# Second batch's transposed x in two PSUM banks, and a new order of the opening, in an attention and MLP kernel

## The chip, the cores and the metric

The kernel runs on one core of one Trainium2 chip. The metric is the device time of one execution in microseconds (us); the time before is the median of three runs. Profiles are of one execution, and times in them count from the start of its span. Engines: PE multiplies matrices, ACT and DVE do element-wise work and copies out of PSUM, POOL does element-wise work in SBUF and issues the loads, SP issues stores and transposing DMAs.

## The reference

```python
B, H, S, Ns, D = (8, 8, 512, 32, 64)
scores = scale * x @ state^T            # softmax over the 32 states
xread  = softmax(scores) @ state        # 512 token rows per batch
scores2 = scale * state @ x^T           # softmax over the 512 tokens
sread  = softmax(scores2) @ x           # 32 state rows per batch
attn   = concatenate([xread, sread], rows), heads side by side   # (8 * 544, 512)
h = attn @ w_in                         # 512 -> 2048
g = maximum(h, 0) + alpha * minimum(h, 0)
out = g @ w_out                         # 2048 -> 512, f32
```

## The kernel before, in words

Everything is computed in f16 with f32 sums. The token rows don't form xread: for each batch, state times w_in is formed first (`state_w_in`, step `m.b.f`, one of four column groups f) and copied to SBUF (`mo.b.f.engine.half`); the softmax weights then multiply it (`first`, step `F.b.jc`, sixteen column blocks jc, two matmuls each; `f.b.jc.g` is one half of such a step, so that it can start when half of the weights are there). `negative` (`N`) on ACT and `prelu` (`G`) on DVE apply the PReLU, and `second` (step `S.b.q.j`, two matmuls each) sums over the blocks with w_out for one of four groups of rows q; `second_out` (`O`) copies the sum and stores it. The state rows of all batches go through `state_reads` (`rd`) and stand as a ninth batch at the end (`F.8.*`, `R`).

Per batch, x is transposed, either by PE (`xt.b.j.g`, four transposes into PSUM, then a copy `xo`; batches 0 and 1) or by a DMA from SP (`xd`; batches 2 to 7). `sc` forms the scores. The softmax over states is `sb` (32x32 transposes, DVE), `smax`, `ssh` (POOL), `sexp` (ACT), `ssum`, `snorm` (POOL), `wb` (DVE, transposes back); F needs `wb`. The softmax over tokens is `tm`, `te` (ACT), `tsum`, `tn` (POOL), `tt` (transposing DMA from SP, read by `rd`). Batch 0 does the first of these in two halves (`sb.0.0`, `sb.0.1`).

Loads are issued on POOL's queue, in its order with its other work: x of batch 0 in halves (`lx0.0`, `lx0.1`), the states of batches 1 to 7 (`lst`), w_in in four column groups (`wi.0` to `wi.3`; `m.b.f` needs `wi.f`), w_out in four row groups (`wo.0` to `wo.3`; `S.b.q.0` and `.1` need `wo.0`, `.2` and `.3` `wo.1`, and so on), x of the later batches (`lx.b`).

The states of batch 0 come by SP, are cast (`stc`), transposed on PE (`stt`, needs the identity `id` that POOL makes) and copied (`sto`); those of the others are transposed in two groups (`str.0`, `str.1`) and copied on ACT (`sro`). `oma` on DVE makes 1 - alpha. `Z.k.n` are filler matmuls of zeros on PE, n units of 128 columns into PSUM bank k, whose result nobody reads.

The order is written out by hand: the string ORDER (L17 to L102) lists the steps, and every engine executes its own steps in that order. A number at the end of a step is the PSUM bank it uses (0 to 5); one further pair of banks ("two") holds `sc` and the `m` without numbers. A step that uses a bank waits until the reader of what stood there is done. The semaphores are set by the framework.

Of the kernel before, what the change touches and what calls it, by code (L numbers as in the profile page):

```python
# [46 lines left out]
S.1.3.5 N.2.8 S.1.3.6 G.2.7 F.2.6.2 O.1.0.a N.2.6 m.3.3.1.0 G.2.8 sc.4 rd.1.5 snorm.p.3 F.2.5.3
G.2.6 mo.3.3.a.0 F.2.14.1 rdo.1.a wb.3 N.2.5 tsum.3 S.2.1.0.2 F.2.11.5 mo.3.3.a.1 G.2.5 S.1.3.7
N.2.14 F.2.10.0 F.3.4.3 G.2.14 N.2.11 S.2.1.1 F.3.1.1 lx.5 O.1.3.v N.3.4 S.2.1.2 N.2.10 G.2.11 tt.2
S.2.0.0.4 S.2.1.3 S.2.0.1 G.2.10 F.3.14.5 F.3.9.0 S.2.1.4 tn.3.1 N.3.1 N.3.9 G.3.1 S.2.1.5 S.2.0.2  # L50
G.3.4 tn.3.0 N.3.14 tm.4 F.3.3.1 F.3.8.3 G.3.14 N.3.8 G.3.9 S.2.1.6 S.2.1.7 S.2.0.3 S.2.3.0.5 N.3.3
xd.5 O.2.1.a tt.3 sb.4 G.3.8 smax.4 F.3.6.0 F.3.2.2 te.4.0 S.2.3.1 S.2.3.2 N.3.6 N.3.2 F.3.13.3
S.2.0.4 te.4.1 ssh.p.4 N.3.13 G.3.3 G.3.6 S.2.0.5 F.3.7.1 G.3.2 S.2.0.6 N.3.7 S.2.0.7 sexp.4 G.3.13
G.3.7 S.2.3.3 S.2.3.4 S.2.3.5 m.6.0 O.2.0.v m.5.1.0.2 mo.6.0.a.1 mo.5.1.a.1 rd.3.3 mo.6.0.v.0
rdo.3.a mo.5.1.v.0 rd.2.1 m.4.1.4.2 ssum.4 sc.5 m.4.3.0.3 rdo.2.a S.2.3.6 mo.4.1.a.1 mo.4.1.a.0 tm.5
tsum.4 snorm.p.4 F.3.5.1 mo.4.3.a.0 mo.4.3.a.1 F.3.0.2 F.3.10.4 N.3.0 S.2.3.7 O.2.3.a S.2.2.0.0
S.2.2.1 F.3.11.3 G.3.0 wb.4 S.2.2.2 S.3.3.0.5 F.3.15.2 S.3.3.1 N.3.5 lx.6 G.3.5 te.5.0 te.5.1 N.3.10
N.3.15 S.2.2.3 F.3.12.1 S.2.2.4 N.3.11 S.3.3.2 lx.7 N.3.12 G.3.10 G.3.15 F.4.6.4 N.4.6 tn.4.0
# [583 lines left out]
```

## Time and profile before

| what | us |
|---|---|
| median of 3 runs (218.33 to 218.44) | 218.37 |
| the profiled execution | 218.92 |
| its span in the profile | 217.1 |
| PE busy in the span | 210.2 |
| DVE busy | 166.7 |
| ACT busy | 137.2 |
| POOL busy | 71.0 |
| matmuls of zeros (L218), busy | 7.3 |

The profile gives a page, and answers to questions about the trace: busy time of every engine in a stretch (windows), what an engine waited for (waits), groups of instructions with count, busy time and mean duration in ns, instructions in order of time (start, duration, engine, line, operation; in brackets the idle time of the engine before it and what ended that), DMA issues with their time to landing, and the chain of work that ended last. PE's matmuls are pipelined: a single one of 512 columns is shown as 379 ns long, but they follow each other more closely, as the chain shows.

### The profile page before, as it was taken

What the parts mean: (1) busy time and instruction counts of PE and PEld (TensorE: products, weight loads), DVE (VectorE), ACT (ScalarE), POOL (GpSimd) and SP (SyncE); (2) the same over time, 40 slices, a digit from 0 to 9 for tenths busy, and PEclk for the clock granted to TensorE, in tenths of its full rate; (3) what the DMA queues carried; (4) which work ended last, traced back from release to release, by engine and by line L of the source; (5) the groups of instructions that cost most, each with busy time, mean ns of one, the idle gap of its engine ahead of it and who ended that gap; (6) DMA issues with size and microseconds to landing.
All of it is one profiled execution on the core that took longest, in us unless ns stands there. A gap on an engine that the chain in (4) does not pass through costs nothing.

```text
span 217.1 us, 4195 instructions
## 1 busy us (share of the span) xinstructions
PE 210.2 (97%) x1637; PEld 99.8 (46%) x1637; DVE 166.7 (77%) x255; ACT 137.2 (63%) x271; POOL 71.0 (33%) x58
## 2 busy tenths in 40 slices
...
DMA packets 39716, 23.12 MB, mean 106 GB/s; under 512 B 22144, under 2 KB 35984, under 8 KB 39696
## 3 DMA queue, kind: packets, MB, share of 16 engines
...
q10 hardware_dynamic: 32, 0.01, 0.0%
...
## 4 chain that ended last, share of the span: by engine, by line
PE 85%; DMA 8%; POOL 2%; DVE 2%; issue 1%; ACT 0%; POOLq 0%
PE o L532 48%; PE h L480 23%; DMA w_in_sb<-in_moe_w_in_dram 6%; PE h L489 3%; PE o L580 3%; PE m_ps L447 3%; DMA st<-in_state_dram 3%; PE o L552 2%; PE sr_ps L422 2%; POOL an L358 1%; PE sc L297 1%; DVE m L469 1%; POOL xg L179 1%; DVE nb L378 1%; POOL w_in_sb L198 0%
## 5 line engine op out<-in xcount | busy, mean ns | idle before, releaser
L532 PE MATMUL o<-w_out_sb,gt 128*128 128x512 f16 x496 | 125.3, 379 | 0.0
L512 ACT ACTIVATE neg<-h 128x512 f32<-128x512 f32 (+1 forms) x144 | 77.0, 579 | 46.9 <-PE h L480 37.4
L520 DVE SCALAR_TENSOR_TENSOR gt<-neg,oma_sb,h 128x512 f16<-128x512 f32 x128 | 89.9, 738 | 15.5 <-ACT neg L512 14.5
L532 PEld LDWEIGHTS <-gt 128*128 128x128 f16 x496 | 47.3, 98 | 55.3 <-issue 3.4
L480 PE MATMUL h<-aT,m 128*128 128x512 f16 x250 | 68.4, 379 | 0.0
L480 PEld LDWEIGHTS <-m 128*128 128x128 f16 x250 | 24.1, 98 | 28.4 <-issue 0.6
L403 POOL TENSOR_SCALAR e<-e,r 128x512 f16<-128x512 f16 x16 | 24.9, 1564 | 20.6 <-DVE r L399 16.7
L469 ACT CAST m<-m_ps 128x512 f16<-128x512 f32 x50 | 27.1, 609 | 4.8 <-PE m_ps L447 4.5
L358 POOL TENSOR_TENSOR an<-ts,r 128x1024 f16<-128x1024 f32 (+1 forms) x9 | 15.4, 1718 | 34.2 <-DVE r L355 14.8
L344 POOL TENSOR_TENSOR ts<-ts,mx 128x1024 f32<-128x1024 f32 (+1 forms) x9 | 15.5, 1719 | 29.0 <-DVE mx L338 29.0
L570 ACT COPY osb<-o 128x512 f32<-128x512 f32 x22 | 12.9, 592 | 14.9 <-PE o L532 14.9
L447 PE MATMUL m_ps<-w_in_sb,stT 64*32 64x512 f16 x256 | 11.4, 383 | 0.8 <-DMA w_in_sb<-in_moe_w_in_dram 0.6
L389 ACT ACTIVATE e<-sc,nb 128x512 f16<-128x512 f32 x16 | 11.1, 703 | 1.1 <-DVE nb L381 1.1
L366 DVE STREAM_TRANSPOSE aT<-an 128x1024 f16<-128x1024 f16 (+1 forms) x9 | 10.1, 1119 | 1.8 <-POOL an L358 1.8
L469 DVE CAST m<-m_ps 128x512 f16<-128x512 f32 x14 | 9.1, 679 | 2.4 <-ACT m L469 1.8
L520 DVE SCALAR_TENSOR_TENSOR gs<-neg,oma_sb,h 128x256 f16<-128x256 f32 x16 | 7.5, 478 | 4.5 <-ACT neg L512 4.5
L378 DVE TENSOR_REDUCE nb<-sc 128x2 f32<-128x1024 f32 x8 | 9.6, 1204 | 0.3 <-PE sc L297 0.3
L338 DVE TENSOR_REDUCE mx<-ts 128x32 f32<-128x1024 f32 (+1 forms) x9 | 9.8, 1092 | 0.0
L354 DVE TENSOR_REDUCE r<-ts 128x32 f32<-128x1024 f32 (+1 forms) x9 | 9.8, 1088 | 0.0
L489 PE MATMUL h<-XS,w_in_sb 128*128 128x256 f16 x64 | 9.4, 273 | 0.0
L590 DVE COPY osr<-o 128x512 f32<-128x512 f32 x1 | 0.7, 691 | 11.3 <-PE o L580 11.3
L218 PE MATMUL z<-zero 128*128 128x512 f16 (+3 forms) x21 | 7.3, 481 | 1.6 <-DVE zero L211 1.3
...
## 6 DMA issues: line engine op xcount, KB each, us to landing
...
xg<-in_x_dram POOLq DMA_DIRECT2D x7, 512.0 KB, 7.0
w_in_sb<-in_moe_w_in_dram POOLq DMA_DIRECT2D x4, 512.0 KB, 9.7
w_out_sb<-in_moe_w_out_dram POOLq DMA_DIRECT2D x4, 512.0 KB, 8.4
...
```

The source lines that it names most:

```text
L344: engine(e).tensor_tensor(ts, ts, over_blocks(cols(live["mx", b], j, S // N)), ALU.subtract)
L358: engine(e).tensor_tensor(blocks(cols(live["an", b], j, S)), blocks(cols(live["ts", b], j, S)), over_blocks(cols(live["r1", b], j, S // N) ...
L378: nc.vector.tensor_reduce(nb, live["sc", b].rearrange("p r j g s -> p g (r j) s"), AX.XY, ALU.max)
L403: nc.gpsimd.tensor_scalar_mul(e2, e2, live["r2", b][:, g : g + 1])
L447: nc.tensor.matmul(t[N * k : N * (k + 1), :], st_head(b, h)[64 * r : 64 * r + 64, :], w_in_sb[64 * r : 64 * r + 64, c, 512 * f : 512 * (f ...
L469: copier(e)(m_tile(b)[:, f, g, :], live["mp", b, f][g])
L480: nc.tensor.matmul(h.rearrange("p (r j s) -> p r j s", r=2, j=2), ms[b][:, f, g, 128 * j : 128 * (j + 1)], weights(b, g), start=(g == 0), ...
L489: nc.tensor.matmul(h, w_in_sb[:, c, 128 * jc : 128 * (jc + 1)], XS[:, c].rearrange("p q n b -> p (q n b)"), start=(c == 0), stop=(c == n_c ...
L512: nc.scalar.activation(neg, h, RELU, bias=0.0, scale=-1.0)
L520: nc.vector.scalar_tensor_tensor(gt, negs.pop((b, jc)), oma_sb[:, jc : jc + 1], h, ALU.mult, ALU.add)
L532: nc.tensor.matmul(outs[b, q], gts[b, jc][:, 128 * q : 128 * (q + 1)], w_out_sb[:, jc, :], start=(jc == 0), stop=(jc == n_jc - 1),)
L570: copier(e)(osb, t)
```

## The change

x of batch 1 is transposed into two PSUM tiles of 1024 f16 columns (one bank each, both j in one) where there were four of 512, and each is copied with one DVE copy (`xo2.1.0.v`, `xo2.1.1.v`) in place of two. The order of all engines is written anew from the start up to about the third batch's first steps; the steps from there on have the same order, with the bank numbers exchanged. In the opening, among others: the identity is made behind `lst` and `wi.0`; `sto` goes to DVE and stands ahead of `oma`; one copy of batch 0's x goes from DVE to ACT; `wo.0` is issued ahead of `ssh.p.0.0`, `wi.2` ahead of both `snorm.p.0`, and `wo.2`, `lx.2` and `wo.3` ahead of `tn.0.0` and `tn.0.1`; `tt.0` is behind three stores on SP; the fillers are 32, 6, 3, 6, 28 and 6 units where they were 24, 13, 6, 3, 7 and 23; `m.4.0` comes ahead of the first `f`.

```diff
@@ ORDER @@
-stc lx0.0 lx0.1 oma id Z.1.24 stt.0 Z.2.13 xt.0.0.0.1 sto.a xt.0.1.0.2 xo.0.0.0.v lst xo.0.1.0.v
-Z.0.6 sc.0.0 xt.0.1.1.3 xt.0.0.1.4 sb.0.0 xo.0.0.1.v smax.0.0 xo.0.1.1.a str.0.5 sc.0.1 str.1.0 wi.0
-sro.0.a lx.1 wi.1 ssh.p.0.0 sb.0.1 Z.1.3 sc.0 Z.5.7 m.0.0.1.2 sro.1.a sexp.0.0 smax.0.1 m.3.0.3.4
-ssh.p.0.1 tm.0 mo.0.0.a.1 sexp.0.1 ssum.0.0 m.1.0.5.0 ssum.0.1 te.0.1 te.0.0 mo.1.0.v.1 wo.0
-mo.1.0.a.0 snorm.p.0.0 mo.3.0.a.1 Z.2.23 xt.1.1.1.2 xt.1.1.0.5 mo.0.0.a.0 snorm.p.0.1 wb.0.0
-mo.3.0.a.0 m.2.0 xt.1.0.1.0 xo.1.1.0.v xt.1.0.0.4 f.0.0.0.1 f.0.1.0.5 wi.2 mo.2.0.a.0 wb.0.1
-mo.2.0.a.1 f.0.1.1 xo.1.0.0.v N.0.1 m.0.1.3.4 f.0.0.1 mo.0.1.a.1 m.1.1 xo.1.1.1.v N.0.0 xo.1.0.1.v
-mo.0.1.v.0 f.0.2.0.2 F.0.3.0 f.0.2.1 F.0.4.3 mo.1.1.v.0 mo.1.1.a.1 F.0.7.4 G.0.1 N.0.2 G.0.0 wo.1
-F.0.5.5 N.0.3 G.0.2 wi.3 m.4.0 N.0.4 S.0.0.0.1 N.0.5 G.0.3 tsum.0 S.0.1.0.2 N.0.7 mo.4.0.a.1 G.0.4
-S.0.0.1 S.0.1.1 G.0.5 mo.4.0.a.0 tn.0.1 m.0.2.0.3 sc.1 G.0.7 S.0.2.0.5 mo.0.2.a.0 tm.1 m.1.2.0.4
-wo.2 tn.0.0 mo.0.2.a.1 mo.1.2.a.0 S.0.2.1 lx.2 wo.3 sb.1 F.0.6.3 F.0.9.0 mo.1.2.a.1 N.0.6 S.0.2.2
-S.0.0.2 N.0.9 G.0.6 S.0.1.2 smax.1 te.1.1 te.1.0 F.0.11.4 G.0.9 ssh.p.1 F.0.8.3 N.0.8 N.0.11 S.0.0.3
-S.0.1.3 m.0.3 G.0.8 F.0.10.0 mo.0.3.a.0 N.0.10 sexp.1 S.0.2.3 mo.0.3.v.1 xd.2 G.0.11 G.0.10
-S.0.3.0.3 m.1.3 S.0.3.1 mo.1.3.a.0 F.0.14.4 S.0.2.4 F.0.13.0 N.0.14 tt.0 ssum.1 S.0.0.4 S.0.1.4
-S.0.0.5 S.0.3.2 G.0.14 F.0.12.4 N.0.13 G.0.13 F.0.15.0 snorm.p.1 N.0.12 N.0.15 mo.1.3.a.1 wb.1
-S.0.3.3 S.0.1.5 S.0.3.4 G.0.12 S.0.2.5 G.0.15 S.0.3.5 F.1.2.4 S.0.2.6 N.1.2 F.1.0.0 tsum.1 S.0.2.7
-N.1.0 S.0.1.6 S.0.1.7 G.1.2 O.0.2.a sc.2 m.2.1.4.5 S.0.0.6 O.0.1.a F.1.7.2 mo.2.1.a.0 mo.2.1.a.1
-G.1.0 F.1.1.0 tm.2 sb.2 F.1.3.4 N.1.7 S.0.0.7 S.0.3.6 N.1.1 G.1.1 N.1.3 tn.1.0 O.0.0.a te.2.0
-F.1.5.5 S.0.3.7 N.1.5 G.1.3 F.1.9.0 S.1.1.0.1 G.1.7 F.1.4.4 smax.2 O.0.3.a S.1.1.1 tn.1.1 G.1.5
-rd.0.2 te.2.1 N.1.9 G.1.9 m.2.3 F.1.6.3 N.1.4 rdo.0.a F.1.12.5 N.1.6 lx.3 G.1.4 F.1.13.2 N.1.12
-F.1.8.0 G.1.6 G.1.12 S.1.2.0.4 N.1.13 G.1.13 ssh.p.2 N.1.8 S.1.1.2 F.1.11.3 G.1.8 F.1.10.5 N.1.11
-S.1.2.1 N.1.10 G.1.11 G.1.10 S.1.2.2 sexp.2 S.1.1.3 ssum.2 F.1.14.2 F.1.15.0 snorm.p.2 mo.2.3.a.0
-S.1.1.4 mo.2.3.a.1 S.1.1.5 m.3.2 m.4.2.3.5 N.1.14 tt.1 tsum.2 N.1.15 G.1.14 mo.3.2.a.1 S.1.1.6
-S.1.2.3 S.1.2.4 mo.3.2.a.0 mo.4.2.a.0 G.1.15 mo.4.2.a.1 S.1.2.5 S.1.1.7 xd.3 O.1.1.a m.3.1.2.0
-m.2.2.3.5 sc.3 wb.2 tn.2.1 S.1.2.6 S.1.2.7 mo.3.1.a.1 F.2.15.1 S.1.0.0.0 mo.2.2.a.0 mo.3.1.a.0
-O.1.2.a lx.4 mo.2.2.a.1 sb.3 N.2.15 S.1.0.1 tm.3 F.2.13.3 N.2.13 G.2.15 S.1.0.2 F.2.4.2 tn.2.0
-F.2.2.4 G.2.13 smax.3 N.2.4 F.2.9.5 F.2.0.1 N.2.9 S.1.0.3 S.1.0.4 G.2.9 S.1.0.5 N.2.2 N.2.0 te.3.0
+lx0.0 lx0.1 lst wi.0 id stc Z.1.32 stt.0 sto.v lx.1 oma wi.1 xt.0.1.0.1 xt.0.0.0.2 xo.0.0.0.v
+xo.0.1.0.a Z.0.6 sc.0.0 xt.0.1.1.3 sb.0.0 xt.0.0.1.4 xo.0.0.1.v xo.0.1.1.a str.1.5 sc.0.1 str.0.0
+wo.0 smax.0.0 ssh.p.0.0 sro.1.a sb.0.1 sro.0.a Z.1.3 sc.0 smax.0.1 Z.5.6 m.1.0.1.2 ssh.p.0.1
+m.0.0.3.4 m.3.0.5.0 sexp.0.0 tm.0 mo.1.0.a.0 mo.1.0.v.1 wi.2 mo.0.0.a.0 ssum.0.0 Z.1.28 xt.1.1.0.1
+mo.0.0.v.1 snorm.p.0.0 mo.3.0.a.1 sexp.0.1 ssum.0.1 m.2.0.3.2 snorm.p.0.1 xt.1.0.0.1 xo2.1.0.v
+wb.0.0 te.0.1 te.0.0 xt.1.1.1.0 mo.2.0.a.1 xt.1.0.1.0 m.4.0 mo.3.0.a.0 wb.0.1 mo.4.0.a.1 Z.2.6
+f.0.0.0.4 xo2.1.1.v wo.1 m.0.1.2.1 mo.2.0.a.0 f.0.2.0.5 mo.4.0.a.0 mo.0.1.a.0 f.0.0.1 f.0.1.0.3
+N.0.0 mo.0.1.v.1 f.0.2.1 f.0.1.1 N.0.1 G.0.0 wi.3 F.0.3.0 G.0.1 N.0.3 F.0.7.2 F.0.5.1 m.1.1 N.0.2
+G.0.3 F.0.4.4 N.0.7 G.0.2 mo.1.1.a.0 S.0.1.0.3 S.0.2.0.0 N.0.5 G.0.7 S.0.2.1 S.0.1.1 m.0.2.5.2
+mo.1.1.a.1 N.0.4 sc.1 mo.0.2.a.0 G.0.5 mo.0.2.a.1 S.0.0.0.1 G.0.4 m.1.2.5.4 S.0.0.1 tm.1 mo.1.2.a.0
+mo.1.2.a.1 F.0.6.2 F.0.9.5 sb.1 S.0.0.2 N.0.6 N.0.9 F.0.11.4 wo.2 G.0.6 te.1.0 S.0.1.2 smax.1
+S.0.2.2 G.0.9 te.1.1 F.0.8.2 lx.2 wo.3 ssh.p.1 S.0.2.3 N.0.11 tsum.1 N.0.8 m.0.3 G.0.11 mo.0.3.a.1
+S.0.1.3 G.0.8 F.0.10.5 mo.0.3.a.0 S.0.0.3 F.0.14.4 m.1.3 N.0.10 G.0.10 S.0.1.4 sexp.1 tsum.0
+F.0.13.2 ssum.1 S.0.2.4 N.0.14 tn.0.0 snorm.p.1 G.0.14 F.0.12.5 N.0.12 S.0.0.4 S.0.1.5 S.0.2.5
+N.0.13 S.0.3.0.4 G.0.12 S.0.3.1 xd.2 F.0.15.5 S.0.0.5 S.0.3.2 mo.1.3.a.1 G.0.13 N.0.15 wb.1 G.0.15
+mo.1.3.a.0 S.0.3.3 F.1.0.2 S.0.2.6 N.1.0 F.1.3.5 N.1.3 S.0.2.7 O.0.2.a S.0.1.6 S.0.1.7 G.1.0 G.1.3
+m.2.1.2.0 sc.2 mo.2.1.a.1 F.1.4.5 O.0.1.a S.0.0.6 sb.2 F.1.12.0 S.0.3.4 F.1.2.3 N.1.4 mo.2.1.a.0
+N.1.2 F.1.1.2 tn.0.1 N.1.1 tm.2 G.1.4 N.1.12 S.0.3.5 S.0.0.7 F.1.5.5 O.0.0.a lx.3 S.0.3.6 tt.0 N.1.5
+G.1.2 xd.3 F.1.9.3 S.0.3.7 F.1.13.1 N.1.9 G.1.12 F.1.6.0 G.1.1 O.0.3.a F.1.8.2 S.1.1.0.4 G.1.9 N.1.6
+F.1.7.3 G.1.5 S.1.1.1 S.1.2.0.5 G.1.6 N.1.8 S.1.2.1 N.1.7 te.2.1 tn.1.1 G.1.8 N.1.13 S.1.2.2
+F.1.11.0 smax.2 te.2.0 F.1.10.2 N.1.11 G.1.7 S.1.1.2 G.1.13 rd.0.3 N.1.10 tn.1.0 m.2.3 S.1.1.3
+rdo.0.a ssh.p.2 F.1.15.1 F.1.14.3 sexp.2 mo.2.3.a.0 G.1.11 mo.2.3.v.1 S.1.2.3 S.1.2.4 S.1.1.4 G.1.10
+S.1.1.5 N.1.15 m.3.2 m.4.2.0.2 S.1.2.5 N.1.14 ssum.2 S.1.1.6 S.1.2.6 G.1.15 mo.3.2.a.1 tt.1
+mo.4.2.a.0 G.1.14 S.1.1.7 snorm.p.2 wb.2 mo.4.2.a.1 mo.3.2.a.0 m.2.2.1.3 m.3.1.0.2 O.1.1.a sc.3
+mo.3.1.a.0 S.1.2.7 mo.2.2.a.0 F.2.15.4 sb.3 tm.3 N.2.15 F.2.13.0 S.1.0.0.1 S.1.0.1 S.1.0.2
+mo.2.2.a.1 O.1.2.a F.2.4.3 mo.3.1.a.1 F.2.9.5 N.2.9 S.1.0.3 G.2.15 smax.3 F.2.2.2 G.2.9 tsum.2
+N.2.13 F.2.0.4 S.1.0.4 N.2.4 S.1.0.5 G.2.13 N.2.2 lx.4 te.3.0 F.2.12.5 G.2.2 ssh.p.3 G.2.4 tn.2.1
...
@@ x_transposed, x_out_both @@
     def x_transposed(b, j, g, k):
-        t = live["xp", b, j, g] = single(k, f"xT_ps{b}_{j}_{g}", [128, 4, 128], F16)
+        if b == 1:
+            if ("xp", b, g) not in live:
+                live["xp", b, g] = single(k, f"xT_ps{b}_{g}", [128, 2, 4, 128], F16)
+            t = live["xp", b, g][:, j]
+        else:
+            t = live["xp", b, j, g] = single(k, f"xT_ps{b}_{j}_{g}", [128, 4, 128], F16)
...
+    def x_out_both(b, g, e):
+        copier(e)(
+            x_tile(b)[:, 4 * g : 4 * g + 4, :, :],
+            live.pop(("xp", b, g)).rearrange("p j h s -> p h j s"),
+        )
...
-        "xd": x_transposed_dma, "xt": x_transposed, "xo": x_out, "sc": scores,
+        "xd": x_transposed_dma, "xt": x_transposed, "xo": x_out, "xo2": x_out_both, "sc": scores,
```

More of the change, by code (lines that the diff above doesn't have):

```diff
@@ L47 @@
[L47 to L58, printed above, removed]
```

102 lines of the change are left out of this document (57 added, 45 removed).

## The prediction

> **What bounds the kernel now.** I read the page first, then busy time by stretch, then DMA issues and instructions in order of time.
>
> ```profile
> span 217.1 us, 4195 instructions
> PE 210.2 (97%) x1637; PEld 99.8 (46%) x1637; DVE 166.7 (77%) x255; ACT 137.2 (63%) x271; POOL 71.0 (33%) x58
> ```
> ```profile
> core 0: us, PE busy (x) PEld busy (x) DVE busy (x) ACT busy (x) POOL busy (x), PEclk, DMA share, GB/s
> 16.00:18.00 2.00, 1.62 (x20) 0.69 (x17) 1.68 (x6) 2.00 (x6) 2.00 (x3) 1.00 1.24 207
> 24.00:26.00 2.00, 2.00 (x17) 0.77 (x16) 1.97 (x3) 1.72 (x4) 1.96 (x2) 1.00 1.24 206
> 34.00:36.00 2.00, 2.00 (x11) 0.88 (x9) 1.17 (x2) 0.39 (x2) 1.91 (x1) 1.00 0.67 109
> 36.00:38.00 2.00, 2.00 (x11) 0.89 (x10) 1.97 (x3) 1.22 (x3) 0.00 (x0) 1.00 0.64 82
> ```
> PE (first pair after the stretch's length) is 97% busy over the span, and full, 2.00 of 2.00, in these stretches from 24 us on. Its work hardly changes with the edit, so the time can move only by PE idling, and the new order reaches only to about 60 us. The loads are the other full resource (last column, GB/s): 207 and 206, drying up at 34 to 38 us. So I list when POOL issues the loads (start, first column), from the DMA view restricted to each its time to landing (last column), and the PE rows that need them.
>
> ```profile
> 5.67 0.77 POOL L198 DMA_DIRECT2D w_in_sb<-in_moe_w_in_dram  x1
> 17.33 0.76 POOL L198 DMA_DIRECT2D w_in_sb<-in_moe_w_in_dram  x1
> 23.73 0.81 POOL L204 DMA_DIRECT2D w_out_sb<-in_moe_w_out_dram  x1
> 26.10 0.94 POOL L162 DMA_DIRECT2D xg<-in_x_dram  x1
> 27.04 0.76 POOL L204 DMA_DIRECT2D w_out_sb<-in_moe_w_out_dram  x1
> ```
> ```profile
> w_in_sb<-in_moe_w_in_dram POOLq DMA_DIRECT2D x1, 512.0 KB, 11.8
> w_in_sb<-in_moe_w_in_dram POOLq DMA_DIRECT2D x1, 512.0 KB, 11.9
> w_out_sb<-in_moe_w_out_dram POOLq DMA_DIRECT2D x1, 512.0 KB, 8.0
> xg<-in_x_dram POOLq DMA_DIRECT2D x1, 512.0 KB, 9.6
> w_out_sb<-in_moe_w_out_dram POOLq DMA_DIRECT2D x1, 512.0 KB, 11.2
> ```
> ```profile
> 17.48 0.41 PE L447 MATMUL m_ps<-w_in_sb,stT 64*32 64x512 f16 x8 [0.38 <-DMA w_in_sb<-in_moe_w_in_dram]
> 29.32 0.41 PE L447 MATMUL m_ps<-w_in_sb,stT 64*32 64x512 f16 x8 [0.20 <-DMA w_in_sb<-in_moe_w_in_dram]
> 38.42 0.59 PE L532 MATMUL o<-w_out_sb,gt 128*128 128x512 f16 x2
> 40.68 0.41 PE L297 MATMUL sc<-xT,stT 64*32 64x256 f16 x16
> 58.52 0.59 PE L480 MATMUL h<-aT,m 128*128 128x512 f16 x2
> ```
>
> Adding the columns: wi.1 lands at 17.47, wi.3 at 29.23, wo.2 at 31.73, lx.2 at 35.70, wo.3 at 38.24. By ORDER the PE rows are m.0.1, m.0.3, S.0.2.6 (the first to read wo.3), sc.2 and F.2.15. m.0.1 and m.0.3 start 0.01 and 0.09 after their weights, and S.0.2.6 only 0.18 after its own. The opening is a row of gates, and PE passes the last weight gate with 0.18 us to spare. What matters is therefore **how much PE work the new order puts ahead of each gate**.
>
> **The change part by part.** Prices:
>
> ```profile
> 36.00 2.16 PE o L532 x10
> ```
> ```profile
> L288 DVE COPY xT<-xT_ps 128x512 f16<-128x512 f16 x7 | 2.7, 407 | 2.3 <-PE xT_ps L283 2.3
> L469 DVE CAST m<-m_ps 128x512 f16<-128x512 f32 x14 | 9.1, 679 | 2.4 <-ACT m L469 1.8 <-PE m_ps L447 0.6
> L354 DVE TENSOR_REDUCE r<-ts 128x16 f32<-128x512 f32 x2 | 1.3, 653 | 0.0
> L366 DVE STREAM_TRANSPOSE aT<-an 128x512 f16<-128x512 f16 x2 | 1.4, 698 | 0.0
> L338 DVE TENSOR_REDUCE mx<-ts 128x32 f32<-128x1024 f32 x7 | 8.5, 1211 | 0.0
> L350 ACT ACTIVATE ts<-ts 128x1024 f32<-128x1024 f32 x7 | 7.4, 1054 | 0.2 <-POOL ts L344 0.2
> ```
>
> A matmul of 512 columns takes 2.16/10 = 0.216 us on the chain, so one step F or S (two of them) is 0.43.
>
> *The merged copies.* Four copies of 407 ns (1.63 us on DVE) become two of 1024 columns. No row has that size. Below: one copy's 407; above: two f32 casts, 2 x 679 = 1358. I take 670: the copy and the cast have the same 512 columns and differ by 272 ns, so I read the copy as 135 ns fixed plus 272, and 1024 columns as 135 + 2 x 272. That frees 1.63 - 1.35 = 0.28 us of DVE. What stands around it costs more:
>
> ```profile
> 9.10 0.58 PE L234 MATMUL st_ps<-ident,st 128*64 128x128 f16 x14 [0.92 <-DMA st<-in_state_dram]
> ...
> 11.35 1.22 DVE L378 TENSOR_REDUCE nb<-sc 128x2 f32<-128x1024 f32 x1
> ...
> 12.60 0.17 DVE L381 TENSOR_SCALAR nb<-nb 128x2 f32<-128x2 f32 x1
> ...
> 13.39 0.25 DVE L355 RECIPROCAL r<-r 128x16 f32<-128x16 f32 x1
> ...
> 16.29 0.81 PE L501 MATMUL h<-aT,m 128*128 128x512 f16 x3
> ...
> 19.23 2.71 DVE L520 SCALAR_TENSOR_TENSOR gt<-neg,oma_sb,h 128x512 f16<-128x512 f32 x4
> ```
>
> *Before 9 us.* The identity moves behind two loads on POOL, first_states_out goes to DVE ahead of oma, and the first filler grows from 24 to 32. PE waited 0.92 us for the states until 9.10, in either order ahead of the second half of the first scores; this covers it. Price 0; if the cover went, all of it would be under 1 us, and the next waits swallow it.
>
> *From 11 to 19 us.* DVE now does, after tm.0 (ends 12.77): cast 0.68, ssum.0.0 0.65 + 0.25, cast 0.68, ssum.0.1 0.90, merged copy 0.67, wb.0.0 0.70: 17.3. So the first first_part matmul starts at 17.3, not 16.29. But m.0.1 waits for wi.1 until 17.48 in both orders, and before it the new order has m.4.0 (early) and only one first_part instead of three. Then wb.0.1 18.0, second copy 18.7, cast mo.0.1.v.1 19.4, and the first G at 19.4 against 19.23: 0.2 late, up to 1.3 with the copies at their upper price. Behind it PE has S.0.1.0, S.0.2.1, m.0.2: they slip by as much, and the wait at m.0.3 takes up to 0.7 of it (next). Price 0, upper end 0.6.
>
> *m.0.3.* S.0.0.3 and S.0.1.3 stood ahead of it, now S.0.2.3 alone: one step, 0.43, moves behind the gate. PE would be there at 28.6 and waits until 29.32. That is +0.43, part of the next term, not added to it.
>
> *S.0.2.6 and wo.3.* Before it the old order has F.1.2, S.0.3.4 and S.0.3.5 more, the new one F.1.0 more. Two steps, 0.86 us of PE work, move behind the gate. PE resumes at 38.24 + 0.04 = 38.28, 0.14 earlier than the 38.42 of before, with 0.86 more to do: **+0.72**.
>
> *The loads themselves.* POOL now issues wo.1, wi.3, wo.2, lx.2 and wo.3 back to back behind snorm.p.0.1 (about 17 to 21 us), past tn.0.0 and tn.0.1; wi.2 goes ahead of both snorm. The order of the ten large loads is the same. As the queue was never empty between 16 and 34 us, an earlier issue gives a longer queue, not an earlier landing: I take landings unchanged. Bounds: lx.2 lands 3.97 after wo.2, wo.3 only 2.54 after lx.2; had lx.2 taken 2.54 as well, wo.3 would land 1.4 earlier, at 36.8. Later by 0.4 at most, as wi.3 is issued at about 17.7 (ssum.0.1 ends at 15.9 by the list above, snorm takes about 1, wo.1's issue 0.8), 0.4 later than before.
>
> [...]
>
> *The transposes.*
>
> ```profile
> xT<-xg SPq DMA_TRANSPOSE x1, 4.4
> ```
>
> sc.2 now comes behind m.2.1; its x lands at 35.70 and is transposed 4.4 later, by 40.2, and PE is there at about 40.9: 0. tt.0 goes behind three stores on SP, the last of them behind the eighth PE step after sc.2 (41.3 + 8 x 0.43 = 44.7, a copy, 45.4), and lands by 49.8. Its reader rd.0 stands 24 steps after sc.2, at 51.7: 0. ACT's te.2.1, which needs the buffer that tt.0 reads, comes at about 49.4 and may hold up N.1.13 by 0.4; that goes into rival (c).
>
> *After sc.2.* The new order puts smax.2 behind eight G:
>
> ```profile
> 46.91 1.91 POOL L344 TENSOR_TENSOR ts<-ts,mx 128x1024 f32<-128x1024 f32 x1 [4.14 <-DVE mx L338]
> ...
> 54.52 1.91 POOL L358 TENSOR_TENSOR an<-ts,r 128x1024 f16<-128x1024 f32 x1 [5.70 <-DVE r L399]
> 56.46 1.25 DVE L366 STREAM_TRANSPOSE aT<-an 128x1024 f16<-128x1024 f16 x1 [0.76 <-POOL an L358]
> 57.80 1.25 DVE L330 STREAM_TRANSPOSE ts<-sc 128x1024 f32<-128x1024 f32 x1
> ```
>
> From sc.2's end at about 41.3: sb.2 and tm.2 1.25 + 1.22 + 0.17, eight G of 2.71/4 = 0.68, smax.2 1.21: 50.6. Shift 1.91 and exponential 1.05: 53.6, while DVE does four G and a cast, 3.4: 54.0. ssum.2 is a reduction of smax.2's size, 1.21, and a reciprocal, about 0.3: 55.5; snorm 1.91, wb.2 1.25: 58.7. F.2.15 needs it; PE is there at 58.52 + 0.72 = 59.24. Cover 0.5, where before had 58.52 - 57.71 = 0.8. Price 0, upper end 0.6.
>
> **Sum.** 218.92 (the profiled execution: span 217.1 and 1.8 around it) + 0.72 = 219.64. The median of the runs, 218.37, lies 0.55 below the profiled execution: 219.1 as a median, 0.3% slower.
>
> **Rivals.**
> (a) *wo.3 lands earlier*, by 0.6 or more, because the longer queue keeps all DMA engines supplied. For: the rate falls from 206 to 109 GB/s before all has landed. Against: wo.3 was issued 11.2 us ahead as it was. The gate then opens before PE comes, but wi.3 still holds 0.43 back, and wb.2 bounds F.2.15 at about 58.7, 0.2 after before: +0 to +0.4, 218.4 to 218.8.
> (b) *Faster*: the start is bound by the issue of loads, not their rate. st and wi.0 are issued about 0.5 us earlier (one identity). If landings followed the issue, the chain st, scores, softmax of the first batch, wb.0.0 and every gate would move 0.5 earlier, and with (a) at the tail no gate holds: 217.9. It decides if wi.1 lands before 17.0 and wo.3 before 37.5. Against: lx0.1 stands in the queue ahead of them, and ACT is full from 16 to 18 us (2.00).
> (c) *Slower still*: the second batch's softmax takes over. wb.2 has 0.5 us of cover in a chain of 17.4 us through DVE, POOL and ACT; 1.1 us longer gives 0.6 on top, 219.7. It decides from wb.2 later than 59.2.
> (d) *The merged copy does not pay*: the rearranged read runs at the cast's rate, 1.36 each. The gate at m.0.3 hides 0.7 of 1.3; the time would be the forecast's or 0.3 more. It is inside the forecast's range.
>
> **How the numbers follow.** Forecast with (d) 0.57, (a) 0.25, (b) 0.07, (c) 0.11. A difference of 0.2%, 0.44 us, is about what a measurement here can tell: 217.93 to 218.81. Slower: (c) and most of the forecast, 0.63; same: (a) and the forecast's low end, 0.29; faster: (b) and a tail of (a), 0.08. The range leaves out (b) and the far part of (c): 218.3, (a) at its best, to 219.6, the forecast with 0.5 of its upper ends.
>
> **What would show it.** Right: PE waits for DMA before the m_ps matmul at about 29.3 for more than 0.5 us, and again, for w_out, about 0.3 us near 38.3; then full to the end; landings within 0.3 us of those above. Wrong: wo.3 landing before 37.6 (a); wi.1's matmul before 17.2 (b); PE idle on DVE's transpose at 59 us (c); copies near 1.3 us (d).

## The result, and the profile after

The changed kernel takes 220.44 us (median of 6 runs, 219.65 to 221.42) where the kernel before takes 218.34 (6 runs beside them, 218.27 to 218.44): a ratio of 1.0093, with a 95% interval from 1.0065 to 1.0121. It is slower, as forecast, but by 2.1 us and not by 0.7, and the time lies outside the range. The profiled execution took 221.42 us, the longest of the six. First its page:

```profile
span 219.7 us, 4193 instructions
PE 211.9 (96%) x1638; PEld 99.8 (45%) x1638; DVE 166.1 (76%) x253; ACT 137.6 (63%) x271; POOL 71.0 (32%) x58
```

PE's work has hardly changed, as expected; the span has grown by 2.6 us. Next the windows of the changed kernel (stretch and its length, busy time and instructions of PE, PEld, DVE, ACT and POOL, granted clock, DMA share, GB/s).

```profile
6.00:8.00 2.00, 0.61 (x10) 0.11 (x8) 1.47 (x5) 0.38 (x1) 1.19 (x2) 0.97 0.97 113
8.00:10.00 2.00, 1.28 (x14) 1.02 (x16) 0.25 (x1) 0.59 (x1) 0.00 (x0) 0.50 1.19 191
10.00:12.00 2.00, 2.00 (x37) 1.41 (x33) 1.60 (x4) 1.17 (x2) 1.05 (x1) 0.50 1.28 183
12.00:14.00 2.00, 2.00 (x27) 0.43 (x34) 1.56 (x2) 1.54 (x2) 1.36 (x2) 0.50 1.42 200
14.00:16.00 2.00, 2.00 (x30) 0.68 (x15) 1.93 (x6) 1.72 (x4) 0.42 (x1) 0.82 1.25 207
...
34.00:36.00 2.00, 2.00 (x11) 0.92 (x10) 1.97 (x4) 1.22 (x3) 1.88 (x2) 1.00 0.97 147
36.00:38.00 2.00, 2.00 (x11) 0.88 (x9) 1.78 (x3) 0.97 (x3) 2.00 (x2) 1.00 0.79 172
```

Two things are new. From 6 to 10 us PE is busy for 1.89 us of 4, and the clock falls to half from about 7.9 to 14.7 us (0.97 of the first stretch and 0.82 of the last: 0.12 + 6 + 0.72 = 6.84 us at half). And at 34 to 38 us the loads run at 147 and 172 GB/s, where the kernel before had 109 and 82. Now POOL, which issues the loads, in order of time, and, from the DMA view of each issue, the time to landing (last column) of wi.3, wo.2, lx.2 and wo.3.

```profile
1.23 1.72 POOL L179 DMA_DIRECT2D xg<-in_x_dram  x2 [0.80 <-POOLq L637]
2.92 0.56 POOL L192 DMA_DIRECT2D st<-in_state_dram  x1
3.46 0.78 POOL L198 DMA_DIRECT2D w_in_sb<-in_moe_w_in_dram  x1
4.20 0.25 POOL masks.py:197 MEMSET ident<- 128x128 f16 x1
...
19.32 0.75 POOL L198 DMA_DIRECT2D w_in_sb<-in_moe_w_in_dram  x1
20.05 0.76 POOL L204 DMA_DIRECT2D w_out_sb<-in_moe_w_out_dram  x1
20.78 0.91 POOL L162 DMA_DIRECT2D xg<-in_x_dram  x1
21.66 0.79 POOL L204 DMA_DIRECT2D w_out_sb<-in_moe_w_out_dram  x1
```
```profile
w_in_sb<-in_moe_w_in_dram POOLq DMA_DIRECT2D x1, 512.0 KB, 8.4
w_out_sb<-in_moe_w_out_dram POOLq DMA_DIRECT2D x1, 512.0 KB, 10.8
xg<-in_x_dram POOLq DMA_DIRECT2D x1, 512.0 KB, 12.6
w_out_sb<-in_moe_w_out_dram POOLq DMA_DIRECT2D x1, 512.0 KB, 14.3
```

Added up, wi.3 lands at 27.7, wo.2 at 30.9, lx.2 at 33.4 and wo.3 at 36.0: 1.5, 0.9, 2.3 and 2.3 us **earlier** than in the trace before, though POOL issues wi.3 two microseconds later than it did. The PE rows that answer to those of before (xt of batch 0's second half, m.0.1, m.0.3, S.0.2.6, F.1.9, F.2.15), and F.1.9 in the kernel before:

```profile
8.68 1.03 PE L288 MATMUL xT_ps<-ident,xg 128*128 128x128 f16 x8 [1.52 <-DMA xg<-in_x_dram]
19.41 0.41 PE L458 MATMUL m_ps<-w_in_sb,stT 64*32 64x512 f16 x8
30.33 0.41 PE L458 MATMUL m_ps<-w_in_sb,stT 64*32 64x512 f16 x8
38.90 0.59 PE L543 MATMUL o<-w_out_sb,gt 128*128 128x512 f16 x2
46.04 0.59 PE L491 MATMUL h<-aT,m 128*128 128x512 f16 x2
61.00 1.04 PE L491 MATMUL h<-aT,m 128*128 128x512 f16 x4 [0.20 <-DVE aT L377]
```
```profile
44.70 0.59 PE L480 MATMUL h<-aT,m 128*128 128x512 f16 x2
```

No weight gate holds PE any more: m.0.3 and S.0.2.6 start 2.6 and 2.9 us after their weights land. The time is lost at two other places. Ahead of m.0.1 stands nearly the same PE work in both orders (0.09 us less in the new one: two halves of F less, m.4.0 more; the fillers, 5 units or some 0.3 us more, are not counted), and it starts 1.93 later: **+2.02 in the opening**. Ahead of F.1.9 and of F.2.15 the work is the same: 46.04 against 44.70 is +1.34, so between m.0.1 and F.1.9 the new order **gains 0.68**; 61.00 against 58.52 is +2.48, so at the third batch it **loses 1.14**. From there to the end the difference stays. This is the chain there, on POOL, ACT and DVE of the changed kernel:

```profile
57.75 1.91 POOL L369 TENSOR_TENSOR an<-ts,r 128x1024 f16<-128x1024 f32 x1 [4.60 <-ACT m L480]
```
```profile
53.18 1.06 ACT L361 ACTIVATE ts<-ts 128x1024 f32<-128x1024 f32 x1
54.14 0.57 ACT L480 CAST m<-m_ps 128x512 f16<-128x512 f32 x1
```
```profile
54.74 0.69 DVE L480 CAST m<-m_ps 128x512 f16<-128x512 f32 x1 [1.62 <-ACT m L480]
55.35 0.74 DVE L531 SCALAR_TENSOR_TENSOR gt<-neg,oma_sb,h 128x512 f16<-128x512 f32 x1
56.01 1.21 DVE L365 TENSOR_REDUCE r<-ts 128x32 f32<-128x1024 f32 x1
...
59.70 1.25 DVE L377 STREAM_TRANSPOSE aT<-an 128x1024 f16<-128x1024 f16 x1 [0.87 <-POOL an L369]
```

DVE idles for 1.62 us ahead of the cast of mo.2.3's second half (`mo.2.3.v.1`), until ACT has cast the first half, which stands behind the exponential on ACT. The row sum ssum.2, whose exponential is ready at 54.24, starts at 56.01 behind that cast and a PReLU, and wb.2 ends at 60.95, the moment F.2.15 starts. In the kernel before both halves of mo.2.3 are ACT's, and they stand behind ssum.2.

The merged copies do what was forecast (instructions, then shortest, median and longest in ns):

```profile
L296 DVE COPY xT<-xT_ps x2: 653/672/692, 17.7 to 19.6; 128x1024 f16<-128x1024 f16 x2
```

### The profile page after: what moved, and what is told of

It reads as the page before. It is cut to its first block, busy times and chain, and to the rows that moved or that the text cites. A ratio compares the mean times of both kernels' runs of the same rounds, so it can differ in the third digit from the quotient of the medians.

```text
span 219.7 us, 4193 instructions
## 1 busy us (share of the span) xinstructions
PE 211.9 (96%) x1638; PEld 99.8 (45%) x1638; DVE 166.1 (76%) x253; ACT 137.6 (63%) x271; POOL 71.0 (32%) x58
## 3 DMA queue, kind: packets, MB, share of 16 engines
q0 software_dynamic: 12704, 8.62, 27.6%
## 4 chain that ended last, share of the span: by engine, by line
PE 89%; DMA 3%; DVE 2%; POOL 1%; ACT 1%; issue 1%; POOLq 0%
PE o L543 48%; PE h L491 24%; PE m_ps L458 4%; PE h L500 3%; PE o L591 3%; DMA st<-in_state_dram 3%; PE o L563 2%; PE sr_ps L433 2%; PE z L218 1%; DVE m L480 1%; PE sc L308 1%; POOL an L369 1%; DVE aT L377 1%; PE st_ps L234 1%; ACT m L480 1%
## 5 line engine op out<-in xcount | busy, mean ns | idle before, releaser
L531 DVE SCALAR_TENSOR_TENSOR gt<-neg,oma_sb,h 128x512 f16<-128x512 f32 x128 | 90.0, 737 | 16.1 <-ACT neg L523 15.2
L458 PE MATMUL m_ps<-w_in_sb,stT 64*32 64x512 f16 x256 | 11.9, 402 | 0.1
L341 DVE STREAM_TRANSPOSE ts<-sc 128x1024 f32<-128x1024 f32 x7 | 8.6, 1232 | 0.5 <-PE sc L308 0.5
```

The costliest lines, as they stand in the source:

```text
L458: nc.tensor.matmul(t[N * k : N * (k + 1), :], st_head(b, h)[64 * r : 64 * r + 64, :], w_in_sb[64 * r : 64 * r + 64, c, 512 * f : 512 * (f ...
L531: nc.vector.scalar_tensor_tensor(gt, negs.pop((b, jc)), oma_sb[:, jc : jc + 1], h, ALU.mult, ALU.add)
```

## The experiments

Kernels beside each other in the table ran on one chip with the kernel before. "Half clock" counts the runs with a mean granted clock under 0.995.

| kernel | median (lowest to highest, runs) | before there | ratio [95%] | half clock |
|---|---|---|---|---|
| the change | 220.44 (219.65-221.42, 6) | 218.34 | 1.0093 [1.0065, 1.0121] | 4 of 6 |
| e1 identity first | 219.49 (219.23-220.43, 12) | 218.47 | 1.0042 [1.0027, 1.0056] | 1 of 12 |
| e2 before, identity late | 218.96 (218.54-220.16, 12) | 218.47 | 1.0016 [0.9998, 1.0035] | 0 of 12 |
| e3 before, tail early | 218.64 (218.22-219.00, 12) | 218.47 | 1.0000 [0.9987, 1.0012] | 0 of 12 |
| e4 change, fillers | 219.89 (219.59-220.72, 6) | 218.47 | 1.0060 [1.0037, 1.0084] | 0 of 6 |
| e5 change, cast on ACT | 219.70 (219.37-220.34, 6) | 218.77 | 1.0052 [1.0035, 1.0069] | 6 of 6 |
| e6 both undone | 218.41 (217.99-218.72, 12) | 218.77 | 0.9986 [0.9974, 0.9998] | 0 of 12 |
| e7 before, cast on DVE | 218.86 (218.52-219.97, 12) | 218.77 | 1.0014 [0.9999, 1.0028] | 1 of 12 |
| e9 e6, x of batch 3 ahead | 219.77 (218.99-220.09, 6) | 218.77 | 1.0049 [1.0032, 1.0067] | 2 of 6 |
| e8 before, merged copies | 218.63 (218.34-219.25, 12) | 218.72 | 0.9978 [0.9954, 1.0003] | 0 of 12 |
| e10 e1, cast later on DVE | 219.29 (218.21-220.33, 12) | 218.72 | 1.0011 [0.9986, 1.0037] | 6 of 12 |
| e11 states, identity, w_in | 219.76 (218.89-220.90, 12) | 218.72 | 1.0036 [1.0010, 1.0063] | 10 of 12 |
| e12 w_in, identity, states | 222.24 (221.33-223.06, 6) | 218.72 | 1.0138 [1.0099, 1.0177] | 6 of 6 |
| e13 e6, identity twice | 218.61 (217.97-221.07, 12) | 218.61 | 1.0017 [0.9986, 1.0047] | 3 of 12 |
| e14 e6, fillers | 218.41 (218.14-218.87, 12) | 218.61 | 0.9994 [0.9982, 1.0005] | 0 of 12 |
| e15 e6 again | 218.45 (217.84-220.44, 12) | 218.61 | 1.0004 [0.9983, 1.0025] | 4 of 12 |

The kernel before had the half clock itself in 1 of 29 runs beside e1 to e4, 0 of 23 beside e5, e6, e7 and e9, 7 of 29 beside e8 and e10 to e12, and 1 of 29 beside e13 to e15.

### The opening: e1, e2, e4

**e1**, the changed kernel with one step moved back:

```diff
-lx0.0 lx0.1 lst wi.0 id stc Z.1.32 ...
+lx0.0 lx0.1 id lst wi.0 stc Z.1.32 ...
```

> The changed kernel with one step moved back: the identity is made ahead of the load of the states and of the first part of w_in, as before. Theory 1 (the time is lost in the first 9 us: the states' load, issued half a microsecond earlier, runs among the second half of batch 0's x, whose last part lands at 8.6 instead of 7.5 us; PE idles and its clock falls): x's second half lands by 7.6 us, granted clock 1.00, and the time falls by 1.3 us or more below the 219.65 of the changed kernel's best runs, to 218.0 to 218.5. Theory 2 (the new order of ACT and DVE from 11 to 19 us costs the 1.3 us that remain in runs with full clock): clock 1.00, but 219.3 to 219.7. The prediction's theory (work moved behind the load gates): 219.0 to 219.2, with PE waiting at 29.3 and 38.3 us.

**e2**, the same exchange in the kernel before (`lst wi.0 id oma` behind `lx0.1`):

> The kernel before with that one step moved alone: the identity behind the load of the states and of the first part of w_in. Theory 1: the second half of batch 0's x lands about 1 us later than 7.5 us, PE falls behind from there, the clock falls in some runs: 219.3 to 221, with a spread of a microsecond or more between runs. Theory 2: no change beyond 0.3 us, since the chain after 9 us is the old one: 218.3 to 218.6.

**e4**, the changed kernel with fillers where PE waits for x:

```diff
-... Z.0.6 sc.0.0 xt.0.1.1.3 ...
+... Z.0.6 sc.0.0 Z.0.24 xt.0.1.1.3 ...
```

> The changed kernel with 24 more units of filler matmuls of zeros on PE between the first half of batch 0's scores and the transposes that wait for the second half of its x, where PE idles. It tells the clock's part from the late load's: if runs with a fallen clock are those in which PE idled there, the granted clock is 0.998 to 1.00 in all runs and the time 219.5 to 219.8, without the runs of 220.4 to 221.4; the late load stays. If the clock falls for another reason: runs of 0.984 to 0.992 as before, 219.6 to 221.4.

e1 takes 0.95 us off the median. That is the time of theory 2, not of theory 1: the opening was about half of the loss, and the rest turned out to lie at the third batch, not between 11 and 19 us as theory 2 has it. In e1's trace PE's transposes start at 7.64, a microsecond earlier than in the changed kernel; its windows beside them are those of the one run of twelve whose clock fell:

```profile
7.64 0.62 PE L288 MATMUL xT_ps<-ident,xg 128*128 128x128 f16 x8 [0.41 <-DMA xg<-in_x_dram]
```
```profile
8.00:10.00 2.00, 1.09 (x27) 0.75 (x24) 1.05 (x3) 0.58 (x1) 0.59 (x1) 0.83 1.18 194
10.00:12.00 2.00, 2.00 (x41) 1.06 (x39) 1.40 (x2) 1.83 (x2) 0.47 (x2) 0.50 1.33 184
12.00:14.00 2.00, 1.76 (x43) 0.53 (x28) 1.62 (x3) 1.56 (x4) 1.75 (x2) 0.82 1.38 195
```

Here the half clock lasts 0.68 + 2 + 0.72 = 3.40 us, half as long as in the changed kernel's trace, and that run took 220.43 where the other eleven took 219.23 to 219.87. The changed kernel's own six runs fall into the same classes: 219.65 and 219.67 at a clock of 0.998 or more, 220.36 to 220.59 at 0.992, 221.42 at 0.984. So one such stretch costs about 0.8 to 0.9 us there.

e4 fills PE's wait: no run had the half clock, though x comes as late as before (its last part at 8.65), and the median is 0.55 below the change. But two of the six runs took 220.53 and 220.72 at full clock. In the trace of the slower one wi.1 lands at 18.7, where the other traces have 17.1 to 18.0, and PE waits 0.59 us for it at m.0.1. The fillers remove the half clock, not the lateness of the loads.

e2 shows the same late x in the kernel before (its last part lands at 8.58 in place of 7.52), but no run had the half clock: PE waits 0.83 us for the late identity, its later work moves with that, and it does not idle for x. m.0.1 starts at 17.62, 0.14 later than before, as the 0.38 that PE waited there for wi.1 is gone. The median is 0.5 above the kernel before, with an interval that still holds no change (0.9998 to 1.0035); the 219.3 or more of theory 1 did not come.

### The tail of the loads: e3, e9

**e3**, the kernel before with the tail issued at once:

```diff
-... wi.3 ... wo.2 tn.0.0 ... S.0.2.1 lx.2 wo.3 sb.1 ...
+... wi.3 wo.2 lx.2 wo.3 ... tn.0.0 ... S.0.2.1 sb.1 ...
```

> The kernel before with the loads wo.2, lx.2 and wo.3 issued right behind wi.3 (ahead of both token normalisations of batch 0), all else as before. If a longer queue makes the tail of the loads land earlier, as the changed kernel's trace suggests: lx.2 lands by about 33.5 instead of 35.7 and wo.3 by 36 instead of 38.2, wi.3 possibly by 28; the time falls by 0.1 to 0.4 us (PE waited 0.2 us at m.0.3 and for nothing at wo.3): 218.0 to 218.3. If the earlier tail comes from something else in the changed order: landings unchanged, 218.3 to 218.4.

The issue of wo.3 in e3, and its time to landing:

```profile
19.75 0.80 POOL L204 DMA_DIRECT2D w_out_sb<-in_moe_w_out_dram  x1
```
```profile
w_out_sb<-in_moe_w_out_dram POOLq DMA_DIRECT2D x1, 512.0 KB, 16.1
```

19.75 + 16.1 = 35.9: wo.3 lands 2.3 us earlier than 38.24. But the longer queue cannot be credited with all of that. e2, e7 and e8 keep the old tail and issue wo.3 as late as the kernel before, at 27.19, 26.94 and 26.97. Their times to landing, in this order, against 11.2 before:

```profile
w_out_sb<-in_moe_w_out_dram POOLq DMA_DIRECT2D x1, 512.0 KB, 9.6
w_out_sb<-in_moe_w_out_dram POOLq DMA_DIRECT2D x1, 512.0 KB, 9.7
w_out_sb<-in_moe_w_out_dram POOLq DMA_DIRECT2D x1, 512.0 KB, 9.4
```

So wo.3 lands at 36.8, 36.6 and 36.4 there, 1.4 to 1.9 us earlier than in the trace that the prediction used, with no longer queue. In the eleven traces with the early tail (e9 and e12, where other loads stand ahead or all are late, left out) it lands at 34.8 to 36.7. The landing scatters from run to run, 38.24 is the latest of the four with the old tail, and what the queue adds (35.9 in e3 against 36.4 to 36.8) is not told apart from that scatter.

e3's time is that of the kernel before, not the 218.0 to 218.3 expected, and S.0.2.6 starts only 0.28 earlier, at 38.14: in the kernel before PE came to this gate 0.18 us after it had opened, so an earlier opening has nothing to give.

**e9** prices the gate itself. It is e6 (below) with lx.3 taken from its later place and put ahead of wo.3:

```diff
-... lx.2 wo.3 ssh.p.1 ... O.0.0.a lx.3 S.0.3.6 ...
+... lx.2 lx.3 wo.3 ssh.p.1 ... O.0.0.a S.0.3.6 ...
```

> The kernel with both undone, and x of batch 3 (512 KB) loaded ahead of wo.3, so that wo.3 lands about 2.5 us later, near 38.4, where the prediction had put it. It prices the prediction's gate: the order of PE is the new one, with two steps more behind that gate. By the prediction's mechanism PE waits for w_out before S.0.2.6 by what it arrives ahead of 38.4, about 0.9 us, and the time is 0.5 to 0.9 above the kernel with both undone. Rival (the gate's wait is given back later, by work that waits for DVE anyway): within 0.2 of the kernel with both undone.

PE's row for S.0.2.6 in e9:

```profile
38.21 0.59 PE L543 MATMUL o<-w_out_sb,gt 128*128 128x512 f16 x2 [1.24 <-DMA w_out_sb<-in_moe_w_out_dram]
```

wo.3 now lands at 38.17, and PE resumes 0.04 behind it, as the prediction had worked out for this gate. S.0.2.6 starts 1.47 later than in e6 (36.74), and the median is 1.36 above e6's. That is more than the 0.5 to 0.9 expected, as PE now comes to the gate earlier; 2 of the 6 runs had the half clock, and the other four alone are 1.25 above e6. The wait is not given back: a gate on this path costs its full length.

### The third batch: e5, e6, e7, e10

**e5** gives the second half of mo.2.3 back to ACT; **e6** is e5 with the identity first as in e1.

```diff
-rdo.0.a ssh.p.2 F.1.15.1 F.1.14.3 sexp.2 mo.2.3.a.0 G.1.11 mo.2.3.v.1 S.1.2.3 ...
+rdo.0.a ssh.p.2 F.1.15.1 F.1.14.3 sexp.2 mo.2.3.a.0 G.1.11 mo.2.3.a.1 S.1.2.3 ...
```

> The changed kernel with the second half of mo.2.3 given back to ACT, so that the cast on DVE and its wait for ACT's first half are gone; the identity stays late. Theory (the added DVE wait makes the third batch's weights late): ssum.2 starts when the exponential ends, about 54.2 in that trace, 1.8 us earlier; wb.2 ends near 59 in place of 60.9; PE no longer waits for DVE before F.2.15, and the loss after m.0.1 shrinks by about 1.1 us: about 1.1 below the changed kernel's 220.4, so 219.3 (218.6 where the clock does not fall in the opening). Rival (what is late there is the whole chain, through the eight PReLUs ahead of smax.2): the time stays within 0.3 of the changed kernel's, and PE still waits for wb.2.

> The changed kernel with both undone: the identity right behind x of batch 0 on POOL, and the second half of mo.2.3 on ACT. Theory (the two losses are separate and add: 1.0 in the opening, 1.1 at the third batch): 219.5 - 1.1 = 218.4, about as before, 217.9 to 218.6. Rival (a third loss takes the place of one of the two): 219 or more, with PE idle at another place after 40 us.

DVE's row sum ssum.2 and its wb.2 in e5:

```profile
53.41 1.22 DVE L365 TENSOR_REDUCE r<-ts 128x32 f32<-128x1024 f32 x1 [0.49 <-ACT ts L361]
...
57.11 1.25 DVE L377 STREAM_TRANSPOSE aT<-an 128x1024 f16<-128x1024 f16 x1 [0.83 <-POOL an L369]
```

ssum.2 now waits for the exponential alone. It starts 2.60 us earlier than in the changed kernel; 0.86 of that is the opening, which was that much shorter in this run (m.2.3 starts at 51.93 in place of 52.79), and 1.74 is the wait. PE's F.2.15 starts at 59.00 without waiting, 0.64 us after wb.2 has ended. The ratio to before falls from 1.0093 to 1.0052 though all six runs had the half clock. In e6 both are undone, and the whole loss goes: 218.41, 0.36 below the kernel before on that chip (ratio 0.9974 to 0.9998; e15 below is the same kernel on another chip, at 0.9983 to 1.0025). e5 and e6 differ in the place of the identity alone and ran on one chip: 219.70 with the half clock in 6 of 6 runs, 218.41 with it in none of 12. The two effects add, within the noise: 0.0051 (e1) and 0.0041 (e5) of the ratio, 0.0092 together, where e6 shows 0.0107.

**e7** puts the same cast on DVE in the kernel before, ahead of ssum.2, with ACT's half right behind the exponential.

> The kernel before with the same cast put on DVE: the second half of mo.2.3 on DVE ahead of ssum.2, and the first half right behind the exponential on ACT, as in the changed kernel. Theory: ssum.2 slips by ACT's half, 0.57, and the cast, 0.68, about 1.25 us in all; 0.8 of it is the cover that wb.2 has before F.2.15 in that trace, so PE waits 0.3 to 0.5 us there: 218.8 to 219.0. Rival (DVE's later work, not the wait, is what costs): within 0.2 of the kernel before.

The cast and wb.2 on DVE in e7:

```profile
52.88 0.69 DVE L469 CAST m<-m_ps 128x512 f16<-128x512 f32 x1 [0.46 <-ACT m L469]
...
57.17 1.25 DVE L366 STREAM_TRANSPOSE aT<-an 128x1024 f16<-128x1024 f16 x1 [0.77 <-POOL an L358]
```

The wait appears here too, but is 0.46 long: DVE has nine PReLUs right ahead of it, and comes to it late. wb.2 ends at 58.42 and F.2.15 starts at 58.47, so the cover is used up and almost nothing more. The time is within the noise of before (ratio 0.9999 to 1.0028); the forecast of 0.3 to 0.5 was too high.

**e10** leaves the cast on DVE, but behind ssum.2 (with the identity first).

> The changed kernel with the identity first, and the second half of mo.2.3 still cast on DVE, but behind ssum.2 in place of ahead of it. Theory (what costs is the place of the wait, ahead of ssum.2, not which engine casts): the same as with the cast on ACT, 218.2 to 218.7. Rival (DVE has no room for this cast anywhere before wb.2): 0.4 or more above that, with PE waiting for DVE before F.2.15.

In its trace ssum.2 starts at 54.12 behind the exponential, wb.2 ends 0.9 us ahead of F.2.15, and PE does not wait there. A smaller wait is new, as m.3.2 waits for the PSUM that the cast now empties later:

```profile
56.32 0.62 PE L458 MATMUL m_ps<-w_in_sb,stT 64*32 64x512 f16 x16 [0.15 <-DVE m L480]
```

From m.0.1 to F.2.15, with the same PE work, e10 takes 40.67 us, e6 40.53 and e1, which has the cast ahead of ssum.2, 41.58: the place of the wait was the cause, not the engine. The medians cannot confirm it to a few tenths: 6 of the 12 runs had the half clock.

### What makes x late: e11, e12, e13, e14, e15

e11 and e12 (both with the cast on ACT) put only one of the two loads ahead of the identity.

```diff
-lx0.0 lx0.1 lst wi.0 id stc ...
+lx0.0 lx0.1 lst id wi.0 stc ...        (e11)
+lx0.0 lx0.1 wi.0 id lst stc ...        (e12)
```

> The changed kernel with the cast on ACT, and the identity behind the states' load but ahead of wi.0. It tells which of the two loads makes the last part of x of batch 0 late. Theory (the loads that are issued within 0.5 us behind lx0.1 share the DMA engines with its last part, and wi.0 with its 512 KB is most of it): x lands near 7.7, 218.4 to 218.9. Rival 1 (the states' load does it, right behind lx0.1): x lands near 8.6 and the time is that of the kernel with the identity behind both, about 219.7, with the half clock in some runs. Rival 2 (the late identity itself holds PE back): the time lies between the two though x lands at 7.6.

> The changed kernel with the cast on ACT, and wi.0 right behind lx0.1, then the identity, then the states' load. Theory (wi.0 makes x late): x of batch 0 lands near 8.6, and the states 0.8 later than with both behind the identity; 219.5 to 220.5. Rival (the states' load does it): x lands near 7.6; then only the states are later, and the time is 218.5 to 219.

Either load does it. PE's transposes start at 8.94 in e11 and at 8.30 in e12 (1.64 and 1.33 us of waiting for x). e12 has its states late besides, PE's row:

```profile
11.91 0.32 PE L234 MATMUL st_ps<-ident,st 128*64 128x128 f16 x2 [2.58 <-DMA st<-in_state_dram]
```

So my theory that wi.0's size was most of it fell, and so did the rival that blamed the states' load alone. What these cases share is that some load is issued at once behind x. A gap does not rule a late part out: with the identity in between, the last part of x comes at 8.45 in e10's trace, and PE waits 1.58 us for it. Then I widened the gap (**e13**: `make_identity` called twice), filled PE's wait (**e14**: `Z.0.24` behind `sc.0.0`, as in e4), and ran e6 beside them (**e15**).

> The kernel with both undone, and the identity made twice, so that 1.1 us in place of 0.55 lie between the issue of the last part of x of batch 0 and that of the next load. Theory (it is the gap that lets the last part land; whatever is issued at once behind it, states or w_in, delays one to three of its 16 parts): no run with the half clock in the opening, x lands by 7.6, and the time is that of the kernel with both undone or up to 0.4 more, as the states and w_in come 0.5 later. Rival (the late parts have nothing to do with what is issued behind them): as many runs with the half clock as with the single identity on this chip.

> The kernel with both undone, and 24 more filler units on PE (1.3 us at full speed) behind the first half of the first scores, where PE waits for x. Theory (the clock is halved when PE idles there, and the half stretch costs 0.8 to 0.9 us): all runs at a granted clock of 0.998 or more, even where x is late; median 218.3 to 218.8, as the fillers themselves may hold the second half of the scores back by up to 0.4. Rival (the fall has another cause): the share of runs with a clock under 0.995 stays that of the kernel without them.

> The kernel with both undone once more, on the chip of these runs, as the reference for the two beside it, and to see whether its time below the kernel before holds on another chip: theory 0.3 to 0.5 below the kernel before in runs with a clock of 0.998 or more, 0.8 above that in runs with the half clock. Rival (the gain belonged to the chip): no difference.

In e13's trace all 16 parts of x have landed by 6.57 us, the earliest of all, and PE does not wait for x. But 3 of its 12 runs had the half clock, beside 4 of 12 for e15: the rival's count. Either the wider gap makes late parts no rarer, or in those runs PE idled for something else, as it does in e13's trace: there it waits 1.36 us for wi.0 ahead of the first m step, at 11.80. I have one trace of e13, and it is not of a run with the half clock. e14 settles the other question. In its profiled run x is late, with its last part at 8.09, but PE is kept busy until 8.6 and the clock stays at 1.00; the rows are PE's, and the window around them:

```profile
7.30 1.47 PE L218 MATMUL z<-zero 128*128 128x512 f16 x6
8.61 0.61 PE L288 MATMUL xT_ps<-ident,xg 128*128 128x128 f16 x8
```
```profile
8.00:10.00 2.00, 2.00 (x36) 1.25 (x36) 0.92 (x3) 0.76 (x2) 0.00 (x0) 1.00 1.20 197
```

All 12 runs of e14 had a clock of 0.998 or more, and its highest time is 218.87, where e15 reached 220.44 on the same chip. e14's median is 0.2 below the kernel before there, which these runs cannot tell from no change (0.9982 to 1.0005). e15's gain over before depends on the clock: its eight runs at 0.998 or more have a median of 218.21, its other four took 218.96 to 220.44.

### The merged copies alone: e8

**e8** is the kernel before with the merged copies, in its own order.

```diff
-... Z.2.23 xt.1.1.1.2 xt.1.1.0.5 mo.0.0.a.0 ... xt.1.0.1.0 xo.1.1.0.v xt.1.0.0.4 ...
+... Z.2.23 mo.0.0.a.0 ... xt.1.0.1.2 xt.1.1.1.2 xo2.1.1.v xt.1.0.0.4 xt.1.1.0.4 ...
-... xo.1.0.0.v ... xo.1.1.1.v ... xo.1.0.1.v ...
+... xo2.1.0.v ...
```

> The kernel before, its order kept, with the two merged copies alone: batch 1's x transposed into bank 2 and bank 4, each copied by one DVE copy; the transposes of a pair stand together. Theory (the copies cost what the prediction said, 0.7 us each in place of two of 0.41, and lie under the wait for w_in): within 0.3 of the kernel before, no wait of PE that is new and over 0.2 us. Rival (holding one bank for two transposes and one long copy stalls the first products of batch 0): 0.4 to 0.8 slower, with PE waiting for xT before 20 us.

The copies take 650 and 692 ns there, and the time is the kernel's before within the noise (218.63, against 218.54 for the 22 runs of the kernel before that had the full clock). So the edit that gives the change its name is neutral; the loss is the order's.

## Why the prediction was wrong

The sign was right by luck: the waits that were to give it did not occur, and two losses priced at 0 did. Step by step:

- ***Before 9 us*, "Price 0": failed**, and it is the larger part in the profiled run. I looked at PE's wait for the states and found it covered, and did not ask what the loads issued 0.5 us earlier would meet. I had the question in hand in rival (b), but only as a gain, with "lx0.1 stands in the queue ahead of them" as if that alone settled when it lands. The runs show x itself landing a microsecond late (8.63 in the changed kernel, 7.52 before), PE idle for 1.52 us, and a clock at half from 7.9 to 14.7 us: 2.02 us in the profiled run, 0.95 of the median by e1, 1.29 between e5 and e6.
- ***The loads themselves*, "I take landings unchanged": failed**, and with it the term +0.72, the whole of the sum. What failed is the figure of the gate: 38.24 was the landing of wo.3 in one trace, and other runs with the same tail have 36.4 to 36.8 (e2, e7, e8). With those the term is nothing even if no landing moves: S.0.2.6 starts at 38.06 in e7, two steps less make it 37.2, and wo.3 is there at 36.6. The 0.43 at m.0.3 hung on such a landing too: wi.3 came at 29.2 there and at 29.4 in e2, but at 27.5 and 27.6 in e7 and e8. In the changed kernel wo.3 landed at 35.9. That is rival (a)'s outcome; that its mechanism, the longer queue, did it is not shown. The working behind the gate was sound: had wo.3 landed at 38.2, PE would have resumed 0.04 later, and the wait would have been paid in full (e9). My argument was that an earlier issue into a queue that is never empty cannot land earlier, but the gate is the last of a load's 16 parts: in the kernel before, 15 parts of wo.3 landed by 36.3 and the last at 38.24. The windows of 109 and 82 GB/s were such late parts, as I read them, and I took them for fixed.
- ***After sc.2*, "Price 0, upper end 0.6": failed**, +1.14 in the profiled run, some 0.9 by e5. Rival (c) had the place and the condition. My chain listed the cast of mo.2.3 among DVE's work, 0.68 us, without the wait that goes with it. The row for it stood in the prediction: `L469 DVE CAST`, idle before it 2.4 us, 1.8 of them until ACT's `m`. I read its duration and not its last column. The rule that I should have followed is that a step given to another engine brings its waits along.
- *From 11 to 19 us*: the price, 0, held where its premise did. Without the late x (e6) the first `f` starts at 16.66 and m.0.1 at 17.18; the list had 17.3 and 17.48, 0.6 and 0.3 too late. *The merged copies*: 0.69 and 0.65 us against 0.67, right; rival (d) is out. *The transposes*: 0, right.
- The stretch from m.0.1 to F.1.9, where the gates stand, became 0.68 us shorter than in the trace before; I had it as longer. Some 0.27 of that is the late wi.3 of that trace: the old order takes 27.22 us for the stretch there and 26.95 in e7 and e8. In the time of the kernel a gain is not shown: e6 is 0.36 below the kernel before on one chip, and e15, the same kernel, is even with it on another.

With the failed terms as measured in the traces, 2.02 - 0.68 + 1.14 gives +2.48 where the sum had +0.72.
